# Strided multiplications of an attention and two-MLP kernel: from two engines by a planner's choice to GpSimd, but for one query step of one tile

## The chip, the cores and the metric

One core of one Trainium2 chip runs the whole program. The metric is device time in microseconds (us) for one execution; the number given for a kernel is the median of several executions. Beside it stands one profiled execution, in which the hardware profiler recorded every instruction with its start, its duration and what released it. The engines are TensorE (PE, with its weight loads PEld), VectorE (DVE), ScalarE (ACT), GpSimd (POOL) and the DMA queues, issued here by SyncE (SP).

## The reference: what is computed

Attention over 4 batches, 8 heads, 576 positions, 64 features, and then two gated MLPs (512 to 1536 to 512) over all 2304 tokens. Half of the heads see a local window of 32 positions, the other half a stride: a position sees the earlier positions (and itself) that are congruent to it modulo 32.

```python
mask_local = (rel >= 0) & (rel < stride)                     # heads 0 to 3
mask_strided = (rel >= 0) & (pos[None, :] % stride == pos[:, None] % stride)   # heads 4 to 7
attn = softmax(where(mask, scale * q @ k.T, -1e9))
x = (attn @ v), tokens as rows
x = ((x @ w_a) * (x @ w_b)) @ w_out                          # first MLP
out = (sigmoid(x @ w_gate) * (x @ w_val)) @ w_out2           # second MLP
```

## The kernel before

The 576 positions are cut into five tiles, `TILES`: four of 128 positions and one of 64, for all four batches at once. They carry the index `i` from 0 to 4.

**Local heads** (`attention`, one group per tile and batch) run on TensorE: scores (L542), then a softmax of small steps, DVE maximum L554 and its scaling L555, ACT exponentials L560, DVE L566 and L567 for the reciprocal of the sums, normalisation on DVE (L575) or ACT (L573), then TensorE transposes (L583) and the product with the values (L597).

**Strided heads** (`strided`, one call per tile) have too few pairs for TensorE: a query step `j` of a tile is 32 positions of four batches on 128 partitions, and it sees only `n = t0 + j + 1` keys. So the scores of one head and one query step are one elementwise multiplication of 128 x (n x 64) (L745, `mult`) into one of two product buffers (ring `p`), and one DVE reduction along the features (L751), which gives the buffer back. After a softmax on the strip `s` (L770 to L784) the values take the same way: a multiplication by the weights (L808) and a DVE reduction along the keys (L815), and at last a transpose on TensorE (L841) and two copies (L854 ACT, L858 DVE). The tiles i = 1 to 4 have n = 5..8, 9..12, 13..16 and 17..18, four heads each: 32, 32, 32 and 16 multiplications, 112 together. Tile 0 takes two heads at a time and is not touched by the change.

**First MLP, first half** ("the loop"): for each tile `i`, 24 products over 512 tokens (256 in the last tile) on TensorE (L887), followed by an ACT copy (L982) and a DVE product (L907) that also frees the PSUM bank. In loop step `i` the attention groups and `strided(i + 1)` of the next tile are worked off beside these products. During the first step the weights of this MLP are prepared too (ACT L464, L481; DVE L473, L485), during the third and fourth step weights of the next stage (DVE L1104, L1040, L1150).

**The order of all work** is written by a planner, `Plan`. Each operation has an engine or a choice of several, a price in ns for each, a key and dependencies. `Plan.run` takes, again and again, the operation that can start first by these prices, and, where engines can be chosen, the one on which it would end first. What comes out is one fixed sequence of instructions per engine, with semaphores; on the chip each engine works its own sequence off in order. TensorE's position for the transposes L583 among the products L887 is thus fixed by the planned times. Each strided multiplication before the change has both engines to choose from:

```python
ways = ("POOL", "DVE")
def price(n):
    n *= nh * D
    return n * 2.05 + 100, dve(n)          # dve(n) = (n + 66) / 0.96
...
m = add(ways, price(n), mult, [lk, lqs[c], m if first else None], w, take=ring("p"))
```

**Second stages**: the rest of the first MLP and the second MLP (L1202 on TensorE, with sums and splits around it on DVE, ACT and a few on POOL, L1040) follow after the loop, from about 412 us on.

Of the kernel before, what the change touches and what calls it, by code (L numbers as in the profile page):

```python
# [173 lines left out]
class Plan:  # L174
# [38 lines left out]
    def add(self, eng, cost, fn, deps=(), key=0.0, take=(), free=(), size=0):  # L213
        op = Op()
        op.slack = self.slack
        op.eng, op.cost, op.fn, op.key, op.size = eng, cost, fn, key * 1e3, size
        op.deps = [d for d in deps if d is not None]
        op.take, op.free, op.slot, op.end = take, free, {}, None
        op.seq = len(self.ops)
        self.ops.append(op)  # L220
        for ring, owner in free:
            if ring in PLACE:
                taker, i = owner if isinstance(owner, tuple) else (owner, None)
                rings = [allowed for r, allowed in taker.take if r == ring]
                for allowed in rings if i is None else rings[i:i + 1]:
                    size = RINGS[ring][1]
                    for s in allowed:
                        a = PLACE[ring] + s * size
                        self.ends.append((a, a + size, op))
        return op  # L230
# [80 lines left out]
def dve(n):  # L311
    return (n + 66) / 0.96
# [27 lines left out]
def attention_moe_kernel(ctx, tc, qkv, sq, sk, sv, w1, w2, mask, ident, out):  # L340
    nc = tc.nc
    PE, ACT, DVE, POOL = nc.tensor, nc.scalar, nc.vector, nc.gpsimd
# [32 lines left out]
    add, touch = plan.add, plan.touch  # L375
# [281 lines left out]
    def strided(i, key, length, start, war):  # L657
        first = i == 0
        tq, t0 = TILES[i] // STRIDE, i * TB // STRIDE
        n1 = t0 + tq  # L660
        nh = 2 if first else 1
        ways = ("POOL", "DVE")
        x = {"q": {}, "xs": {}, "ps": {}}
        step = [0]

# [1 line left out]
            step[0] += 1  # L667
            return key + length * step[0] / (2 * HL // nh * tq + 4)

        def price(n):  # L670
            n *= nh * D
            return n * 2.05 + 100, dve(n)


        rings = {"q": ("c", F_RING), "strip": ("raw", (0, 1, 2)), "p": ("p", (0, 1))}
# [3 lines left out]
        def place(op, use, w):  # L679
            if first:  # L680
                return at(*op.early)[:, :w]
            return {"c": small, "raw": raw, "qk": qk_buf, "p": product_buf}[rings[use][0]](op)[:, :w]

        def ring(use):
            return [] if first else [rings[use]]
# [26 lines left out]
        def own_tile(op):  # L712

            if first:
                op.early = early_tile()
                touch(op, (), [op.early])
            return op
# [7 lines left out]
        lqs, reds, m = [], [], None  # L725
        for h in range(0, HL, nh):
            c, e = divmod(h, 2)
            if e == 0:
                def load_q(op, c=c):
                    q = place(op, "q", 2 * tq * D)  # L730
                    nc.sync.dma_start(
                        out=q.rearrange("p (h x) -> p h x", h=2),
                        in_=sq[:, 2 * c:2 * c + 2, t0 * D:n1 * D],
                    )
                    x["q"][c] = q.rearrange("p (h t d) -> p h t d", h=2, d=D)

                lqs.append(own_tile(add("SP", 450, load_q, start, key - 10, take=ring("q"),
                                        size=P * 2 * tq * D * 4)))
            lk = own_tile(add("SP", 450, load_strip(sk, "k", h), start, key - 9 + h * length / 8,
                              take=ring("strip"), size=P * nh * n1 * D * 4))  # L740
            for j in range(tq):
                n = t0 + j + 1

                def mult(op, h=h, e=e, j=j, n=n):
                    engine[op.eng].tensor_tensor(  # L745
                        out=product(op, n), in0=x["k", h][:, :, :n, :],
                        in1=x["q"][h // 2][:, e:e + nh, j:j + 1, :].to_broadcast([P, nh, n, D]),
                        op=ALU.mult)

                def reduce(op, h=h, j=j, n=n):  # L750
                    DVE.tensor_reduce(  # L751
                        out=weights_of(h, j, n), in_=x["p", op.deps[0]], op=ALU.add, axis=AX.X)

                w = when()
                m = add(ways, price(n), mult, [lk, lqs[c], m if first else None], w, take=ring("p"))
                reads(own_tile(m), lk, lqs[c])
                free = freed("p", m)
                if j == tq - 1:
                    free += freed("strip", lk) + (freed("q", lqs[c]) if e + nh == 2 else [])
                reds.append(reads(add("DVE", dve(nh * n * D), reduce, [m, fi], w, free=free), m))  # L760
# [28 lines left out]
        w = when()  # L789
# [4 lines left out]
        o5 = add("DVE", dve(ns), normalise, [o4], w, free=[("sm", o1)])  # L794
        for h in range(0, HL, nh):
            c, e = divmod(h, 2)
            lv = own_tile(add("SP", 450, load_strip(sv, "v", h, STEPS[i], "p (h d t) -> p h d t"), start, key - 9 + (h + 4) * length / 8,
                              take=ring("strip"), size=P * nh * n1 * D * 4))
            for j in range(tq):
                n = t0 + j + 1  # L800

                if first and e == 0 and j == 0:
                    xs_at = early_tile()

                def mult(op, h=h, e=e, j=j, n=n, xs_at=xs_at):
                    if e == 0 and j == 0:
                        x["xs"][h // 2] = at(*xs_at)[:, :tq * P] if first else place(op, "q", tq * P)
                    engine[op.eng].tensor_tensor(  # L808
                        out=product(op, n, "p (h d t) -> p h d t"), in0=x["v", h][:, :, :, :n],
                        in1=weights_of(h, j, n).unsqueeze(2).to_broadcast([P, nh, D, n]),  # L810
                        op=ALU.mult)

                def reduce(op, h=h, e=e, j=j, n=n):
                    xs = x["xs"][h // 2].rearrange("p (t h d) -> p t h d", h=2, d=D)
                    DVE.tensor_reduce(  # L815
                        out=xs[:, j, e:e + nh, :], in_=x["p", op.deps[0]], op=ALU.add, axis=AX.X)

                w = when()
                take = ring("p")
                if e == 0 and j == 0:  # L820
                    take += ring("q")
                m = add(ways, price(n), mult, [lv, o5, m if first else own], w, take=take)
                reads(own_tile(m), lv)
                if e == 0 and j == 0:
                    own = m
                free = freed("p", m)
                if j == tq - 1:
                    free += freed("strip", lv)
                    if h + nh == HL:
                        free.append(("s", fi))  # L830
                red = reads(add("DVE", dve(nh * n * D), reduce, [m, own], w, free=free), m)
                if first:
                    touch(red, (), [xs_at])
                parts[c].append(red)
            if e + nh < 2:
                continue

            def transpose(op, c=c):
                x["ps"][c] = bank(op)
                for j in range(tq):  # L840
                    PE.transpose(  # L841
                        x["ps"][c][:, j * P:(j + 1) * P], x["xs"][c][:, j * P:(j + 1) * P], idt)

            def views(c):
                w = TILES[i]
                o = (i % 2) * N2
                return [x["ps"][c][:, :tq * P].rearrange("p (t b r) -> p t b r", b=B, r=STRIDE)] + [
                    xT(y, 2)[:, c, o:o + B * w].rearrange("p (b t r) -> p t b r", b=B, r=STRIDE)
                    for y in range(2)
                ]  # L850

            def high(op, c=c):
                ps, hi, lo = views(c)
                ACT.copy(out=hi, in_=ps)  # L854

            def low(op, c=c):
                ps, hi, lo = views(c)
                DVE.tensor_tensor(out=lo, in0=ps, in1=r32(hi), op=ALU.subtract)  # L858

            tr = add("PE", tq * 109, transpose, parts[c] + [c_id], w,  # L860
                     take=[("bank", tuple(range(8)) if first else (4, 5, 6, 7))], free=freed("q", own))
            if first:
                touch(tr, [xs_at])
            hi = add("ACT", act(tq * P), high, [tr] + war, w)
            lo = add("DVE", dve(tq * P), low, [hi], w, free=[("bank", tr)])
            outs.setdefault(i, {}).setdefault(2 + c, []).append((hi, lo))
# [77 lines left out]
    for i, n in enumerate(TILES):  # L944
        n *= B
        war = reads1[-1:]
        w = [g for g in GROUPS if g.i == i + 1]
# [9 lines left out]
        for k in range(KF):  # L957
# [4 lines left out]
            ring = "c" if last and k % 2 else "g"  # L962
# [476 lines left out]
    for s in range(KS):  # L1439
# [5 lines left out]
        i, k = ((2, 0), (2, 6), (3, 0), (3, 3), (3, 6), (3, 9))[s]  # L1445
# [92 lines left out]
```

## Time and profile before

| | us |
|---|---|
| median of 3 executions | 957.09 (957.0 to 958.74) |
| profiled execution | 956.21 |
| its span, first to last instruction | 954.40 |
| PE busy in the span | 904.0 (95%) |
| DVE busy | 709.2 (74%) |
| ACT busy | 427.3 (45%) |
| POOL busy | 150.9 (16%) |

The span is what the trace shows; 1.81 us of the profiled execution lie around it. Busy shares are means over stages with different limits: the loop, where DVE, POOL and PE work beside each other, and the stages after it, where PE works nearly without a gap. A PE instruction counts as busy from its start to its modelled end. The granted clock is 1.00 at 2.4 GHz and 0.50 at 1.2 GHz, and stands as a mean over a stretch.

### The profile page before, as it was taken

What the parts mean: (1) busy time and instruction counts of PE and PEld (TensorE: products, weight loads), DVE (VectorE), ACT (ScalarE), POOL (GpSimd) and SP (SyncE); (2) the same over time, 40 slices, a digit from 0 to 9 for tenths busy, and PEclk for the clock granted to TensorE, in tenths of its full rate; (3) what the DMA queues carried; (4) which work ended last, traced back from release to release, by engine and by line L of the source; (5) the groups of instructions that cost most, each with busy time, mean ns of one, the idle gap of its engine ahead of it and who ended that gap; (6) DMA issues with size and microseconds to landing.
All of it is one profiled execution on the core that took longest, in us unless ns stands there. A gap on an engine that the chain in (4) does not pass through costs nothing.

```text
span 954.4 us, 14300 instructions
## 1 busy us (share of the span) xinstructions
PE 904.0 (95%) x5170; PEld 826.2 (87%) x5170; DVE 709.2 (74%) x1101; ACT 427.3 (45%) x883; POOL 150.9 (16%) x101
## 2 busy tenths in 40 slices
PE   5898999979888899999999979999999999999998
PEld 3676777767666678999999979999999999999998
DVE  6999799798979984565859997666566656748591
ACT  4655332214132243334537575555566555435351
POOL 4324335452424510000000221000000000000000
PEclk9999999989999999999999999999999999999999
DMA  9576653455357556994343641537366668954401
GB/s 296 186 265 202 208 158 104 153 150 184 102 177 214 185 167 208 390 361 148 137 157 127 228 150 56 198 125 236 133 213 225 198 234 309 400 176 148 155 11 66
DMA packets 95349, 179.91 MB, mean 189 GB/s; under 512 B 9520, under 2 KB 66480, under 8 KB 93616
## 3 DMA queue, kind: packets, MB, share of 16 engines
q1 hardware_dynamic: 94992, 178.80, 56.1%
q8 instruction: 40, 0.66, 0.3%
q10 hardware_dynamic: 288, 0.21, 0.1%
q14 instruction: 29, 0.24, 0.1%
HBM read 120.78 MB, written 58.20 MB: 188 GB/s over the span
## 4 chain that ended last, share of the span: by engine, by line
PE 74%; DVE 14%; issue 4%; DMA 3%; ACT 2%; POOL 2%; SPq 0%; DVEq 0%; ACTq 0%; POOLq 0%
PE bank L1202 55%; PE bank L887 16%; DVE s L751 2%; DVE rest L815 2%; DVE w9p L745 1%; DVE h16p L907 1%; PE bank L583 1%; DVE rest L473 1%; DMA rest<-w 1%; POOL w9p L745 1%; PE bank L597 1%; DMA rest<-sq 1%; DMA w10p<-w 1%; PE bank L542 1%; DVE w10p L1104 1%
## 5 line engine op out<-in xcount | busy, mean ns | idle before, releaser
L1214 DVE TENSOR_TENSOR rest<-bank,rest 128x384 f32<-128x384 f32 x96 | 52.8, 554 | 76.5 <-PE bank L1202 44.1
L1220 ACT COPY rest<-bank 128x384 f32<-128x384 f32 x96 | 46.0, 479 | 94.3 <-PE bank L1202 94.0
L808 POOL TENSOR_TENSOR w9p<-rest,s 128x448 f32<-128x448 f32 (+13 forms) x37 | 67.8, 1842 | 90.4 <-DVE rest L815 58.2
L745 POOL TENSOR_TENSOR w9p<-rest 128x384 f32<-128x384 f32 (+11 forms) x30 | 55.2, 1845 | 103.0 <-DVE s L751 52.3
L982 ACT COPY h16p<-bank 128x512 f32<-128x512 f32 (+1 forms) x54 | 30.3, 561 | 70.1 <-PE bank L887 60.5
L751 DVE TENSOR_REDUCE s<-w9p 128x8 f32<-128x512 f32 (+13 forms) x57 | 50.5, 904 | 1.9 <-POOL w9p L745 1.7
L907 DVE TENSOR_TENSOR h16p<-bank,h16p 128x512 f32<-128x512 f32 (+1 forms) x54 | 35.2, 653 | 22.1 <-PE bank L887 17.3
L815 DVE TENSOR_REDUCE rest<-w9p 128x64 f32<-128x320 f32 (+13 forms) x56 | 49.9, 907 | 1.4 <-POOL w9p L808 1.4
L560 ACT ACTIVATE rest<-bank,nm 128x96 f32<-128x96 f32 x56 | 18.3, 339 | 59.3 <-DVE nm L555 53.5
L583 PE MATMUL bank<-idt,rest 128*96 128x128 f32 x56 | 12.2, 324 | 29.2 <-DVE rest L575 20.5
L583 PEld LDWEIGHTS bank<-idt,rest 128*96 128x96 f32 x56 | 7.0, 139 | 35.7 <-issue 15.7
L745 DVE TENSOR_TENSOR w9p<-rest 128x704 f32<-128x704 f32 (+11 forms) x26 | 33.4, 1289 | 6.1 <-DMA rest<-sk 4.4
L1224 ACT COPY bank<-bank 128x384 f32<-128x384 f32 x48 | 22.3, 465 | 25.8 <-PE bank L1202 25.3
L1097 ACT ACTIVATE rest<-rest 128x512 f16<-128x512 bf16 x36 | 28.1, 789 | 6.3 <-DMA rest<-w 6.1
L1049 ACT CAST w10p<-rest 128x768 fp32r<-128x768 f32 (+1 forms) x30 | 23.4, 813 | 16.7 <-DVE rest L1040 16.7
L1421 ACT COPY rest<-bank 128x384 f32<-128x384 f32 x24 | 11.5, 481 | 40.9 <-PE bank L1202 40.9
L1104 DVE SCALAR_TENSOR_TENSOR rest<-rest 128x512 uint32<-128x512 uint32 x36 | 25.4, 708 | 4.7 <-ACT rest L1097 4.7
L1285 DVE TENSOR_TENSOR rest<-bank,rest 128x384 f32<-128x384 f32 x36 | 20.0, 555 | 11.5 <-PE bank L1202 11.2
L1279 ACT ACTIVATE rest<-bank 128x384 f32<-128x384 f32 x36 | 17.8, 493 | 21.1 <-PE bank L1202 21.0
L808 DVE TENSOR_TENSOR w9p<-rest,s 128x768 f32<-128x768 f32 (+10 forms) x19 | 24.3, 1280 | 0.5
L1202 PE MATMUL bank<-w10p,w5p 128*128 128x384 f32 x120 | 23.7, 335 | 0.0
L464 ACT ACTIVATE rest<-rest 128x512 f16<-128x512 bf16 x24 | 18.8, 789 | 7.5 <-DMA rest<-w 7.5
(584 smaller groups left out, 2716.3 us busy)
## 6 DMA issues: line engine op xcount, KB each, us to landing
rest<-w SPq DMA_DIRECT2D x60, 511.8 KB, 4.3
h2d<-rest SPq DMA_DIRECT2D x18, 768.0 KB, 4.4
w1d<-w11p SPq DMA_DIRECT2D x72, 128.0 KB, 1.8
h1d<-h16p SPq DMA_DIRECT2D x36, 192.0 KB, 2.2
w10p<-w SPq DMA_DIRECT2D x12, 511.8 KB, 5.1
rest<-qkv SPq DMA_DIRECT2D x12, 416.0 KB, 4.3
w0p<-h1d SPq DMA_DIRECT2D x12, 384.0 KB, 5.5
w1p<-h1d SPq DMA_DIRECT2D x12, 384.0 KB, 5.8
```

The lines of the kernel that those rows point to most:

```text
L583: PE.transpose(x["t"][:, i * P:(i + 1) * P], blocks(x["e"])[:, i, :], idt)
L745: engine[op.eng].tensor_tensor(out=product(op, n), in0=x["k", h][:, :, :n, :], in1=x["q"][h // 2][:, e:e + nh, j:j + 1, :].to_broadcast([P ...
L751: DVE.tensor_reduce(out=weights_of(h, j, n), in_=x["p", op.deps[0]], op=ALU.add, axis=AX.X)
L808: engine[op.eng].tensor_tensor(out=product(op, n, "p (h d t) -> p h d t"), in0=x["v", h][:, :, :, :n], in1=weights_of(h, j, n).unsqueeze(2 ...
L815: DVE.tensor_reduce(out=xs[:, j, e:e + nh, :], in_=x["p", op.deps[0]], op=ALU.add, axis=AX.X)
L887: PE.matmul(x[tag][:, :n], ww[:, c * P:(c + 1) * P], xx(c), start=(u == 0 and c == chunks[0]), stop=(u == last and c == chunks[-1]),)
L907: DVE.tensor_tensor(out=x["g"], in0=x["b"][:, :n], in1=x["g"], op=ALU.mult)
L982: ga, mu = gated(x, key, n, pa, pb, lambda o, a: ACT.copy(out=o, in_=a), ring)
L1104: DVE.scalar_tensor_tensor(out=u, in0=u, scalar=13, in1=at(*top_at, U32), op0=ALU.logical_shift_right, op1=ALU.bitwise_or)
L1202: PE.matmul(bank_of(where), at(*lhs(a, (0, 1, 0)[q], c), F32R), at(*rhs(b, (0, 0, 1)[q], c), F32R), start=p in OPENS and (q, c) == units[0 ...
L1214: DVE.tensor_tensor(out=at(*o), in0=bank_of("Z"), in1=at(*a), op=ALU.add)
L1220: "ACT", act2(NS), lambda op: ACT.copy(out=at(*o), in_=bank_of("Y")), [ops[after]], key - 20))
```

## The change

In the tiles i = 1 to 4 every strided multiplication is given to POOL alone, at a planned price of 2.5 ns an element and 100 ns, and no longer chosen by the planner. The exception is the second query step (j = 1, n = 14, 896 elements) of tile i = 3, whose eight multiplications (four heads, scores and values) are given to DVE alone. Tile 0 keeps its choice and its prices. Since prices and engines are inputs of the planner, the sequences of all engines are planned anew.

```diff
-        ways = ("POOL", "DVE")
...
-        def price(n):
+        def by(n, j):
+
             n *= nh * D
-            return n * 2.05 + 100, dve(n)
+            if first:
+                return ("POOL", "DVE"), (n * 2.05 + 100, dve(n))
+            return ("DVE", dve(n)) if i == 3 and j == 1 else ("POOL", n * 2.5 + 100)
...
-                m = add(ways, price(n), mult, [lk, lqs[c], m if first else None], w, take=ring("p"))
+                m = add(*by(n, j), mult, [lk, lqs[c], m if first else None], w, take=ring("p"))
...
-                m = add(ways, price(n), mult, [lv, o5, m if first else own], w, take=take)
+                m = add(*by(n, j), mult, [lv, o5, m if first else own], w, take=take)
```

## Rows read from the trace of the kernel before

**Rows 1.** Windows: length, PE, PEld, DVE, ACT, POOL busy (instructions), clock, DMA share, GB/s
```profile
26.00:111.00 85.00, 76.46 (x415) 59.11 (x414) 78.90 (x132) 47.29 (x100) 33.35 (x28) 0.94 0.63 202
111.00:176.00 65.00, 62.72 (x366) 48.23 (x365) 56.88 (x86) 17.58 (x62) 25.07 (x16) 1.00 0.52 157
176.00:281.00 105.00, 92.17 (x504) 72.07 (x503) 94.60 (x120) 28.49 (x82) 38.95 (x19) 0.93 0.47 145
281.00:345.00 64.00, 57.28 (x275) 44.42 (x274) 59.57 (x74) 18.24 (x49) 27.54 (x10) 0.95 0.61 193
...
412.00:954.00 542.00, 533.06 (x3023) 530.79 (x3021) 363.43 (x566) 279.31 (x488) 16.28 (x11) 1.00 0.53 181
```

**Rows 2.** Waits of PE from 26 to 412 us: total, times, longest
```profile
PE bank L583 <- DVE rest L575: 20.5, 6, 4.8
PE bank L583 <- ACT rest L573: 8.7, 4, 4.2
```

**Rows 3.** Timeline of PE around one such wait: start, duration, idle before
```profile
241.94 0.61 PE L887 MATMUL bank<-x13p,w3p 128*128 128x512 f32 x2
246.24 0.96 PE L583 MATMUL bank<-idt,rest 128*96 128x128 f32 x4 [3.69 <-DVE rest L575]
246.85 1.20 PE L887 MATMUL bank<-x12p,w3p 128*128 128x512 f32 x2
```

**Rows 4.** Timeline of DVE and POOL: start, duration, what it is
```profile
189.37 1.99 POOL L745 TENSOR_TENSOR w9p<-rest 128x832 f32<-128x832 f32 x1 [2.22 <-DVE s L751]
...
190.34 0.67 DVE L907 TENSOR_TENSOR h16p<-bank,h16p 128x512 f32<-128x512 f32 x1
...
236.74 2.39 POOL L808 TENSOR_TENSOR w9p<-rest,s 128x1024 f32<-128x1024 f32 x1 [4.07 <-DVE rest L815]
...
237.16 2.00 DVE L555 TENSOR_SCALAR nm<-nm 128x4 f32<-128x4 f32 x1
...
330.36 0.17 DVE L555 TENSOR_SCALAR nm<-nm 128x2 f32<-128x2 f32 x1
```

**Rows 5.** Windows, multiplications L745 alone: DVE busy, POOL busy (instructions)
```profile
26.00:111.00 85.00, 3.33 (x4) 14.57 (x12) 0.94 0.63 202
111.00:176.00 65.00, 9.23 (x10) 9.70 (x6) 1.00 0.52 157
176.00:281.00 105.00, 13.30 (x8) 19.14 (x8) 0.93 0.47 145
281.00:345.00 64.00, 7.50 (x4) 11.77 (x4) 0.95 0.61 193
```

**Rows 6.** The same windows, multiplications L808 alone
```profile
26.00:111.00 85.00, 2.09 (x3) 18.38 (x14) 0.94 0.63 202
111.00:176.00 65.00, 8.73 (x7) 15.05 (x9) 1.00 0.52 157
176.00:281.00 105.00, 11.41 (x8) 18.65 (x8) 0.93 0.47 145
281.00:345.00 64.00, 2.55 (x2) 15.77 (x6) 0.95 0.61 193
```

**Rows 7.** Groups by shape, 26 to 345 us on DVE, all of POOL: busy, mean ns
```profile
L808 DVE TENSOR_TENSOR w9p<-rest,s 128x896 f32<-128x896 f32 x1 | 1.1, 1087 | 0.0
...
L808 POOL TENSOR_TENSOR w9p<-rest,s 128x896 f32<-128x896 f32 x3 | 7.2, 2403 | 19.4 <-DMA rest<-qkv 14.4 <-DVE rest L815 4.9
```

**Rows 8.** Groups by shape on DVE, 26 to 345 us: busy, mean ns, idle before
```profile
L473 DVE SCALAR_TENSOR_TENSOR rest<-rest 128x512 uint32<-128x512 uint32 x23 | 19.9, 868 | 0.7 <-ACT rest L464 0.7
L555 DVE TENSOR_SCALAR nm<-nm 128x4 f32<-128x4 f32 x11 | 6.4, 579 | 0.4
L566 DVE TENSOR_SCALAR nm<-nm 128x4 f32<-128x4 f32 x12 | 4.8, 396 | 0.7 <-ACT rest L560 0.7
...
L485 DVE SCALAR_TENSOR_TENSOR w3p<-rest,w3p 128x512 fp32r<-128x512 f32 x3 | 2.0, 680 | 0.0
```

**Rows 9.** Windows, weight preparation L485 alone: DVE busy (instructions)
```profile
26.00:111.00 85.00, 22.22 (x24) 0.94 0.63 202
```

## The prediction

> **What bounds the kernel now.** I read the windows first, cut where one strided tile ends and the next begins. From 412 us on PE is busy 533.06 of 542 us [rows 1]: no work on DVE or POOL can be worth much there, and the change touches none of it. So the answer lies in the four stretches of the loop, 26 to 345 us. In 111 to 176 PE is busy 62.72 of 65 us at full clock; in the three others it lacks 8.5, 12.8 and 6.7 us, and the granted clock is 0.94, 0.93 and 0.95. The engine that is nearly full there is DVE: 78.90 of 85, 94.60 of 105 and 59.57 of 64 us [rows 1], while POOL works 33.35, 38.95 and 27.54 us. I take DVE for the limit of these three stretches, PE for that of the second.
>
> The waits of PE say through which door: ten waits, 29.2 us, all before the transposes L583, that is for a normalised softmax of the local heads (20.5 us by DVE, 8.7 us by ACT, whose input, in the code, comes from DVE's L567) [rows 2]. TensorE's order is fixed, so a softmax that is later than the planner thought stops it. One such wait stands in the timeline: 3.69 us idle before 246.24, and the pair of products behind it takes 1.20 us where the pair before the wait took 0.61 [rows 3]: the clock fell to its lower level. The clock's shares are 0.06 x 85 + 0.07 x 105 + 0.05 x 64 = 15.7 us [rows 1], in part of idle time that is counted already. What can be won in the loop is therefore at most some 45 us.
>
> Why DVE is late is seen where it works beside POOL [rows 4]. L555, a step on 4 elements, takes 0.17 us alone, but 2.00 us when it starts at 237.16 within a POOL multiplication (236.74, 2.39 us): both end within 0.1 us. L907, which reads PSUM, takes 0.67 us in the middle of a POOL multiplication. So some DVE steps wait until the POOL instruction in flight is done, and all that stands behind them in DVE's sequence waits too; reductions and reads of PSUM don't.
>
> **Part 1: multiplications that leave DVE.** By the windows DVE does 4 + 2, 10 + 7, 8 + 8 and 4 + 2 of them in the tiles 1 to 4, 45 together, and POOL 67 of the 112 (of the three L808 in the first stretch one is the last of tile 0) [rows 5, 6]. Their DVE time: 3.33 + 2.09 - 0.68 = 4.7 us (0.68 for tile 0's, a 512-element step [rows 8]); 9.23 + 8.73 = 18.0; 13.30 + 11.41 = 24.7; 7.50 + 2.55 = 10.0; together 57.4 us. After the change eight remain, in tile 3, of 896 elements at 1.09 us [rows 7] = 8.7 us. DVE is relieved of 48.7 us: 4.7, 18.0, 16.0 and 10.0. The reductions stay as they are.
>
> **Part 2: multiplications that POOL gets.** Net 6, 17, 8 and 6, 37 together. POOL's mean in each stretch is (14.57 + 18.38) / 26 = 1.27 us, 24.75 / 15 = 1.65, 37.79 / 16 = 2.36 and 27.54 / 10 = 2.75 [rows 5, 6], so it gets 7.6 + 28.0 + 18.9 + 16.5 = 71 us more and is busy 41 of 85, 53 of 65, 58 of 105 and 44 of 64 us. That fits, tightest in the second stretch. POOL's time costs nothing by itself while it hides beside the products of TensorE; if that cover were gone, the rival on POOL below says what it costs. Of an instruction of 896 elements POOL needs 2403 ns, DVE 1087 [rows 7].
>
> **Part 3: waits that grow.** POOL is in flight in the loop 190 us instead of 123, so DVE's hindered steps meet it more often. What they lose now, over the undisturbed 0.68 us of L485 and 0.17 us of L555 (for L566 too) [rows 4, 8]: L473 19.9 - 23 x 0.68 = 4.3; L485 22.22 - 24 x 0.68 = 5.9 [rows 9]; L555 6.4 - 11 x 0.17 = 4.5; L566 4.8 - 12 x 0.17 = 2.8 us [rows 8]. The first two, 10.2 us, fall upon the 26 POOL multiplications of tile 1, 0.39 us for each; the last two, 7.3 us, upon all 67, 0.11 us for each. So a POOL multiplication costs DVE 0.11 us where no weights are prepared (tile 2) and about 0.5 us where they are (tile 1; tiles 3 and 4 prepare others, which I price alike). Added: 6 x 0.5 + 17 x 0.11 + 8 x 0.5 + 6 x 0.5 = 12 us. The lower end is 37 x 0.11 = 4 us. The upper end is a hindered step for each added multiplication, which waits for half of it: 71 / 2 = 35 us. I take 12, since it comes from the same steps of the same tiles, only more often hit.
>
> The Trainium skill, page "SBUF — State Buffer", section "SBUF: two separate sides", says that VectorE and GpSimd share a pair of ports as an exclusive lock, held for the whole instruction, and that the loser is blocked fully. L555's 2.00 us agree. By that rule the worst case is each added instruction's whole length in front of a waiting DVE step, as an estimate 71 us instead of the 12 taken, and the change would lose.
>
> **Part 4: the sum.** DVE's net relief is 4.7 - 3 = 1.7 us in tile 1, 18.0 - 1.9 = 16 in tile 2, 16.0 - 4 = 12 in tile 3 and 10.0 - 3 = 7 in tile 4. Not all of it reaches the end. In tile 2 PE lacks only 2.3 us [rows 1]. Elsewhere the planner sees the shorter DVE work too and puts the transposes nearer to their scores, which uses up part of it; what surely shrinks is lateness carried from one softmax to the next. Between nothing and all I take a third: 0.5 (tile 1), 0.5 (tile 2), 4 (tile 3) and 2 (tile 4) = 7 us. The clock comes back in the proportion of the waits, 15.7 x 7 / 29.2 = 4 us, of which I count half, since part of it is idle time counted already: 2 us. 9 us from the profiled execution's 956.2 us (span 954.4 and 1.8 around it) gives 947 us; the median of the runs is 0.9 us above that execution, so 948 against 957.1.
>
> A new plan also moves what it does not mean to move: the clearing of buffers (L1079) queues on POOL behind multiplications, the strips and their DMAs on SP's queue are freed when a multiplication that reads them ends, now later on the slower engine, and the next strip load and all loads planned behind it on that queue move with it. I cost these at nothing: POOL keeps idle time in each stretch [rows 1] and covers them. If that cover is gone (tile 2), it is 2 to 3 us of a strip load's lateness, inside the range.
>
> **Rivals.**
>
> *Lateness goes entirely.* With 49 us less to do, DVE catches up before each softmax, and only each softmax's own waits are left. For it: lateness adds up now, DVE being full at 90% and more. Against it: L555 and L566 lie in the chain itself and are hit more often. If about 20 of the 29.2 us and half of the clock's share as before go: 956 - 25 = 931 us; between this and the likeliest lies 938. Chance 0.14.
>
> *No change.* What DVE is relieved of sits in tile 2, where PE was full, and in the other tiles the waits eat the rest: 957 us. For it: tile 1 had 26 of its 32 multiplications on POOL already, and it waits no less. Within 0.2% (1.9 us), which is about what a measurement here can tell from nothing. Chance 0.12.
>
> *Slower through the lock.* The softmax steps on DVE (L555, L566, and L575) are just of the hindered kind; with POOL in flight 60% of the loop, 190 of 319 us, each of some 14 softmaxes in it meets a POOL instruction more often, for half of 2.4 us. One more hit each is 14 x 1.2 = 17 us on the path of the transposes, less the 9 us of relief: 8 us slower, 965 us. It decides when an added multiplication costs DVE more than 48.7 / 37 = 1.3 us. For it: 2.00 us for L555. Against it: on the whole trace a POOL multiplication costs these two steps only 0.11 us. The skill's lock rule above is the ground of this rival. Chance 0.17.
>
> *GpSimd too late.* In tile 2 POOL would have 53 us of multiplications in 65, in series with the softmax of the strip between them and with waits for DVE; at 0.4 us more for each of 32 that is 66 us. Then the strided half of the next tile's input is late, each later tile starts later, and PE waits before a tile's first product: some 5 us, 961 us. It decides when tile 2's multiplications take more than its stretch. Chance 0.07.
>
> **How the numbers follow.** Likeliest, 948 (941 to 955): 0.50. Entirely without lateness: 0.14. No change: 0.12. Lock: 0.17. GpSimd late: 0.07. Faster by over 0.2%: 0.50 + 0.14 = 0.64; within: 0.12; slower: 0.17 + 0.07 = 0.24. The range reaches from 935, in the middle of the second case, to 963, which leaves out about 0.07 below and 0.11 above: the lower end is also a gain of two thirds instead of one third in tiles 3 and 4 with more clock, the upper end the added waits near 35 us.
>
> **What would show it.** Right: DVE's L745 and L808 only in tile 3, eight of 1.0 to 1.1 us; POOL's busy time about 71 us more, mean durations unchanged; PE's waits before L583 from 29 to some 20 us; the stretch of tile 3 several us shorter, that of tile 2 the same length; from 412 us on the same length. Wrong: L555 and L566 at 1 us and more in the mean, POOL waiting for nothing in tile 2 and the first products of a tile behind L841, or waits of PE of the old size at other places, which would mean that their cause is the planner's distance and not DVE's load.

## The result and the profile after

The changed kernel takes 948.5 us (median of 5, 946.01 to 951.54) against 957.55 us for the kernel before; the ratio is 0.9906 with a 95% interval of 0.988 to 0.9932. The forecast was 948 us. The number was met, but, as the experiments show, by another way than the one that I had worked out.

The lines of the program stand two lower after the change: L745 is L747, L751 is L753, L808 is L810, L815 is L817, L887 is L889, L907 is L909, L1104 is L1106.

The profiled execution (948.5 us, span 946.7) by windows, cut again where a strided tile ends, with the columns of [rows 1]:

```profile
26.00:109.00 83.00, 75.17 (x417) 58.14 (x418) 75.94 (x124) 48.06 (x103) 40.98 (x34) 0.98 0.63 203
109.00:183.00 74.00, 69.39 (x404) 54.47 (x403) 47.85 (x74) 17.51 (x57) 52.55 (x33) 0.95 0.48 141
183.00:283.00 100.00, 93.92 (x509) 73.02 (x507) 88.01 (x112) 29.05 (x84) 56.98 (x27) 0.98 0.50 158
283.00:355.00 72.00, 63.06 (x312) 48.43 (x313) 67.03 (x82) 23.04 (x65) 41.80 (x16) 0.95 0.63 208
```

The stretch of tile 2, the second, is 74 us long in place of 65. POOL is busy 53 us of it, and DVE 47.85 us, in [rows 1] 56.88 of 65. The waits of PE from 26 to 412 us, as in [rows 2]:

```profile
PE bank L583 <- DVE rest L575: 12.8, 6, 3.7
PE bank L583 <- ACT rest L573: 11.1, 5, 4.1
PE bank L597 <- ACT rest L589: 1.5, 2, 0.9
PE bank L843 <- DVE rest L817: 1.1, 1, 1.1
```

Before the transposes 29.2 us of waits have become 23.9. The groups that answer to [rows 7, 8], on DVE from 26 to 355 us (busy, mean ns):

```profile
L747 DVE TENSOR_TENSOR w9p<-rest 128x896 f32<-128x896 f32 x4 | 8.8, 2211 | 0.1
L566 DVE TENSOR_SCALAR nm<-nm 128x4 f32<-128x4 f32 x12 | 8.4, 702 | 0.6 <-ACT rest L560 0.5
L555 DVE TENSOR_SCALAR nm<-nm 128x4 f32<-128x4 f32 x11 | 6.8, 618 | 0.4
L810 DVE TENSOR_TENSOR w9p<-rest,s 128x896 f32<-128x896 f32 x4 | 6.3, 1568 | 0.1
```

and of the whole trace the multiplications on POOL (page part 5):

```profile
L747 POOL TENSOR_TENSOR w9p<-rest 128x320 f32<-128x320 f32 (+12 forms) x52 | 94.0, 1828 | 76.6 <-DVE s L753 42.2
L810 POOL TENSOR_TENSOR w9p<-rest,s 128x320 f32<-128x320 f32 (+12 forms) x52 | 96.6, 1881 | 63.3 <-DVE rest L817 36.7
```

Where the time comes from is read off the timeline of PE. Each step of the loop runs from the start of its first instruction L887 to that of the next step's (step 0 from its second one, at 27.1 to 29.4 us); the last column is where the next stage's first product starts. The kernels with an underscore are those of the experiments below:

```
                 step 0   step 1   step 2   step 3   step 4   loop ends at
before            90.6     80.4     94.5     82.7     34.4      411.43
after             88.3     83.7     86.2     83.7     34.4      404.73
e1_tile3          89.9     81.8     85.1     80.1     34.4      400.00
x1_engines        90.2     85.2     92.8     85.3     34.4      417.32
x2_order          88.8     80.4     91.4     82.7     34.4      406.63
b7_nolock         88.5     80.1     91.4     81.3     34.4      402.89
e1_7_nolock       88.8     80.5     78.8     75.5     34.4      386.98
```

Of the 7.7 us between the two spans 6.7 lie ahead of the loop's end: 0.6 before its products, 2.3 in step 0, 8.2 in step 2, while steps 1 and 3 lose 3.4 and 1.0. Behind the loop the program takes 543.0 and 541.9 us.

### The profile page after: what moved, and what is told of

Same layout as the page of the kernel before. It is cut to its first block, busy times and chain, and to the rows that moved or that the text cites. A ratio compares the mean times of both kernels' runs of the same rounds, so it can differ in the third digit from the quotient of the medians.

```text
span 946.7 us, 14276 instructions
## 1 busy us (share of the span) xinstructions
PE 900.0 (95%) x5170; PEld 823.5 (87%) x5170; DVE 691.1 (73%) x1063; ACT 428.2 (45%) x885; POOL 218.3 (23%) x138
## 4 chain that ended last, share of the span: by engine, by line
PE 76%; DVE 11%; DMA 5%; issue 3%; ACT 2%; POOL 2%; SPq 1%; DVEq 0%; POOLq 0%; ACTq 0%
PE bank L1204 55%; PE bank L889 18%; DMA h1d<-h16p 1%; DMA rest<-w 1%; DVE h16p L909 1%; DVE s L753 1%; PE bank L583 1%; PE bank L597 1%; DVE rest L473 1%; DVE rest L817 1%; POOL w9p L810 1%; DVE rest L575 1%; DMA rest<-sk 1%; POOL w9p L747 1%; DVE nm L566 1%
## 5 line engine op out<-in xcount | busy, mean ns | idle before, releaser
L747 POOL TENSOR_TENSOR w9p<-rest 128x320 f32<-128x320 f32 (+12 forms) x52 | 94.0, 1828 | 76.6 <-DVE s L753 42.2
L810 POOL TENSOR_TENSOR w9p<-rest,s 128x320 f32<-128x320 f32 (+12 forms) x52 | 96.6, 1881 | 63.3 <-DVE rest L817 36.7
L753 DVE TENSOR_REDUCE s<-w9p 128x8 f32<-128x512 f32 (+13 forms) x57 | 51.0, 905 | 12.9 <-POOL w9p L747 12.7
L817 DVE TENSOR_REDUCE rest<-w9p 128x64 f32<-128x320 f32 (+13 forms) x56 | 50.4, 910 | 11.2 <-POOL w9p L810 11.0
L909 DVE TENSOR_TENSOR h16p<-bank,h16p 128x512 f32<-128x512 f32 (+1 forms) x54 | 35.3, 653 | 22.9 <-PE bank L889 9.5
L583 PE MATMUL bank<-idt,rest 128*96 128x128 f32 x56 | 11.7, 307 | 24.0 <-DVE rest L575 12.8
L583 PEld LDWEIGHTS bank<-idt,rest 128*96 128x96 f32 x56 | 6.6, 132 | 30.6 <-issue 14.9
L1051 ACT CAST w10p<-rest 128x768 fp32r<-128x768 f32 (+1 forms) x30 | 23.4, 812 | 18.1 <-DVE rest L1042 18.1
L1099 ACT ACTIVATE rest<-rest 128x512 f16<-128x512 bf16 x36 | 28.1, 788 | 6.3 <-DMA rest<-w 6.0
L1423 ACT COPY rest<-bank 128x384 f32<-128x384 f32 x24 | 11.5, 481 | 40.9 <-PE bank L1204 38.2
L1106 DVE SCALAR_TENSOR_TENSOR rest<-rest 128x512 uint32<-128x512 uint32 x36 | 24.5, 685 | 5.3 <-ACT rest L1099 5.3
L1042 POOL TENSOR_TENSOR rest<-w0p,rest 128x384 f32<-128x384 f32 x1 | 1.0, 1016 | 102.2 <-DVE w8p L1053 102.2
L473 DVE SCALAR_TENSOR_TENSOR rest<-rest 128x512 uint32<-128x512 uint32 x24 | 20.8, 870 | 1.1 <-ACT rest L464 1.1
L1149 ACT ACTIVATE w11p<-w11p 128x256 fp32r<-128x256 f32 x24 | 9.9, 416 | 25.5 <-DVE w11p L1042 13.2
```

Source lines behind the costliest of these rows:

```text
L473: DVE.scalar_tensor_tensor(out=u, in0=u, scalar=13, in1=x["t"], op0=ALU.logical_shift_right, op1=ALU.bitwise_or,)
L747: engine[op.eng].tensor_tensor(out=product(op, n), in0=x["k", h][:, :, :n, :], in1=x["q"][h // 2][:, e:e + nh, j:j + 1, :].to_broadcast([P ...
L753: DVE.tensor_reduce(out=weights_of(h, j, n), in_=x["p", op.deps[0]], op=ALU.add, axis=AX.X)
L810: engine[op.eng].tensor_tensor(out=product(op, n, "p (h d t) -> p h d t"), in0=x["v", h][:, :, :, :n], in1=weights_of(h, j, n).unsqueeze(2 ...
L817: DVE.tensor_reduce(out=xs[:, j, e:e + nh, :], in_=x["p", op.deps[0]], op=ALU.add, axis=AX.X)
L909: DVE.tensor_tensor(out=x["g"], in0=x["b"][:, :n], in1=x["g"], op=ALU.mult)
```

## The experiments

The theories. *DVE relief* is that of the prediction: DVE was full, 49 us of multiplications less let it keep up. *Price*: a planned POOL price nearer to the chip's gives a better order. *Reshuffling*, later *order*: the change's worth is that all sequences are planned anew, and the one before was poor. *Distance*: transposes are planned too near to their scores. *Lock in the chain*: the softmax's own small DVE steps, waiting for POOL, make the waits. Each ratio is against runs of the kernel before on the same chip.

**Tile by tile.** `e1_tile3`, `e2_tile2` and `e3_not_tile2` use the new rule for some tiles alone, `e4_price` only the new price:

```diff
-            if first:
+            if first or i != 3:        # e1_tile3; i != 2: e2_tile2; i == 2: e3_not_tile2
                 return ("POOL", "DVE"), (n * 2.05 + 100, dve(n))
...
-            return ("DVE", dve(n)) if i == 3 and j == 1 else ("POOL", n * 2.5 + 100)
+            return ("POOL", "DVE"), (n * 2.5 + 100, dve(n))       # e4_price alone
```

> Only tile i = 3 has the new rule (POOL, but j = 1 on DVE); tiles 1, 2 and 4 choose as before. Theory 'DVE relief, tile by tile': the whole gain sits in the third loop step, whose length fell from 94.5 to 86.2 us, so this kernel has it alone: 949 to 950 us against 957.5. Rival 'price': the gain comes from a planned POOL price that is nearer to the chip, in all tiles; one tile of four gives a quarter to a third of it, about 955 us. Rival 'reshuffling': any new plan moves the time by some us without order, 953 to 961 us.

Measured: 943.61 us, ratio 0.9857 (0.9831 to 0.9883): more than the whole change gives, and not in step 2 alone; step 3, whose tile chose as before, is 2.6 us shorter too.

> Only tile i = 2 has the new rule (all 32 multiplications on POOL). Theory 'DVE relief, tile by tile': PE was full there, relief is worth nothing, and the second loop step gets about 3 us longer as in the changed kernel (80.4 to 83.7 us) with a wait of some 3.7 us before L583: about 960.5 us. Rival 'price': faster, about 955 us. Rival 'reshuffling': 953 to 961 us, with the loss or gain in other steps than the second.

Measured: 951.53 us, ratio 0.9934 (0.991 to 0.9957). Faster, where the relief could be worth nothing; step 1 did get longer (83.1 us), but step 2, with the rule before, got 3.7 us shorter (90.8 us; the profiled execution, 955.27 us, is the slowest of the six).

> The changed kernel, but tile i = 2 chooses as before. Theory 'DVE relief, tile by tile': the loss in the second loop step is avoided and the gains of the others stay: about 945 us, 3 us below the changed kernel. Rival 'price': a part of the gain is lost, about 951 us. Rival 'reshuffling': 943 to 955 us without relation to the steps.

Measured: 945.41 us, ratio 0.9863 (0.9839 to 0.9886), as DVE relief expected, but the loss that it should avoid is there: step 1 takes 85.5 us with the old choice.

> The engines stay the planner's choice, only the POOL price is 2.5 ns an element and 100 ns instead of 2.05. Theory 'DVE relief, tile by tile': the planner now gives DVE more multiplications, not fewer, DVE is fuller and its softmax steps later: 960 to 965 us. Rival 'price': the order fits the chip better, about 950 us.

Measured: 945.29 us, ratio 0.9864 (0.9837 to 0.989). DVE has more multiplications than before (56 of the tiles' 112, not 45), up to the loop's end it is as busy (327.99 us, 327.70 in the kernel before), and the kernel is as fast as the best of these. Its windows of L747 and L810 (DVE busy, POOL busy) in the stretch from 176 to 281 us:

```profile
176.00:281.00 105.00, 10.99 (x9) 17.36 (x7) 0.97 0.48 147
...
176.00:281.00 105.00, 11.29 (x10) 16.01 (x6) 0.97 0.48 147
```

19 of 32 on DVE, and yet a step 2 of 86.0 us. DVE relief as the cause falls with this run. The effects of single tiles don't add up either, and show in steps that were not touched.

**Price or any new order.** `n1_210` and `n2_200` change one digit of the kernel before; `e5_price205` is the changed kernel with the old price; `m1_800` gives the planner 400 ns more for each hop in the local softmax:

```diff
-            return n * 2.05 + 100, dve(n)
+            return n * 2.10 + 100, dve(n)      # n1_210;  n * 2.00 + 100: n2_200
...
-            ... else ("POOL", n * 2.5 + 100)
+            ... else ("POOL", n * 2.05 + 100)  # e5_price205, in the changed kernel
...
-M1, M2 = 400, 50
+M1, M2 = 800, 50                               # m1_800
```

> The kernel before with one number changed: the planned POOL price 2.10 instead of 2.05 ns an element, engines still the planner's choice. Theory 'price' (the gain grows as the planned price nears the chip's): a ninth of the way to 2.5, 956 us. Theory 'DVE relief': a few multiplications more on DVE, 957.5 us or a little above. Theory 'reshuffling' (the sequence before is one of many that differ by chance in how their waits before L583 fall, and it is a poor one): several us away from 957.5, anywhere from 944 to 960 us.

Measured: 947.82 us, ratio 0.9878 (0.9865 to 0.9892).

> The kernel before with the planned POOL price 2.00 instead of 2.05 ns an element. Theory 'price': away from the chip's, 958 to 960 us. Theory 'DVE relief': a few multiplications more on POOL, 956 to 957 us. Theory 'reshuffling': several us away from 957.5 without regard to the direction, 944 to 960 us.

Measured: 957.75 us, ratio 0.998 (0.9968 to 0.9991).

> The changed kernel, the same engines for every multiplication, but the POOL price as before, 2.05 ns an element. Theory 'DVE relief': the engines make the gain, 948 us. Theory 'price': the gain goes, 957 us or more, since each multiplication is planned to end 0.3 us too early. Theory 'reshuffling': 944 to 960 us.

Measured: 948.83 us, ratio 0.9886 (0.9873 to 0.99). A price that is nearer to the chip's is not it: the old price with the new engines is as good as the changed kernel, and 2.5% on the price of the kernel before, with engines still chosen, gives more than 1% of time. The waits of `n1_210`:

```profile
PE bank L583 <- ACT rest L573: 11.6, 7, 3.6
PE bank L583 <- DVE rest L575: 10.9, 5, 3.4
```

22.5 us in place of 29.2, though DVE does as much work: 327.74 us up to the loop's end, 327.70 in the kernel before. `n2_200` gains almost nothing, so not every new order helps: the times scatter from 944 to 958 us, and the sequence before stands at their slow end.

> The kernel before with one number changed: the slack M1 that the planner adds to each hop between engines in the local heads' softmax is 800 ns instead of 400, so that the transposes L583 are planned some 2 us later behind more products of TensorE. Theory 'distance' (what costs time is TensorE standing at a transpose that was planned nearer than the chip's softmax takes, with the low clock behind it, not a full DVE): waits before L583 fall from 29 to 12 us, 940 to 945 us. Theory 'DVE relief': DVE is full, the wait moves elsewhere, 955 to 958 us.

Measured: 955.68 us, ratio 0.9957 (0.9944 to 0.9971). TensorE had more work between scores and transposes, 40 instructions L887 in place of 28 for the softmax whose scores end at 200 us, but it still waited 7.2 us there: from scores to transposes it was 17.6 us in place of 11.5. DVE's sequence fills the room with other steps. The waits before L583 are 25.3 us in all (16.3 and 9.0), where 12 were expected. At this one value, distance fails.

**Engines and order apart.** Both kernels leave the planner alone and only issue the multiplication on another engine than it planned; the sequences of TensorE and ACT, and those of DVE and POOL but for the multiplications, are then, instruction for instruction, those of the kernel whose order they have. `x1_engines` has the order before and the engines after, `x2_order` the reverse:

```diff
-                    engine[op.eng].tensor_tensor(                     # L745 and L808, planner of before
+                    engine["DVE" if i == 3 and j == 1 else "POOL"].tensor_tensor(       # x1_engines, tiles 1 to 4
...
-                    engine[op.eng].tensor_tensor(                     # L747 and L810, planner of after
+                    engine["DVE" if (i, v, h, j) in ON_DVE else "POOL"].tensor_tensor(  # x2_order: the 45 of before
```

> The planner's order of the kernel before, for TensorE, ACT and all other instructions alike, but each strided multiplication of tiles 1 to 4 is issued on the engine that the changed kernel gives it (POOL, but j = 1 of tile 3 on DVE). Engines alone, no new order. Theory 'DVE relief': the engines make the gain, 948 us or a little better. Theory 'order' (the gain is the new order's, whatever the engine): 957 us; if the added POOL time only brings waits, 960 to 970 us.

Measured: 959.17 us, ratio 1.0009 (0.9992 to 1.0027): engines alone are worth nothing. Up to its loop's end, and for the kernel before, the windows say (columns of [rows 1]):

```profile
26.00:417.32 391.32, 356.51 (x1997) 284.69 (x1997) 293.36 (x450) 135.79 (x345) 191.00 (x110) 0.95 0.59 189
```

```profile
26.00:411.43 385.43, 355.05 (x1996) 283.42 (x1994) 327.70 (x485) 135.13 (x345) 124.90 (x73) 0.96 0.60 192
```

DVE is relieved by 34 us, and the loop takes 6 us more in this execution (960.87 us, 1.7 above the median of its kernel; that of the kernel before, 956.21 us, is below its own). The waits of PE are 33.6 us:

```profile
PE bank L583 <- DVE rest L575: 20.0, 6, 6.9
PE bank L583 <- ACT rest L573: 13.6, 4, 6.1
```

And DVE, with less to do, stands before its reductions until POOL's multiplications are done, 44.1 us in the loop (L754 and L818 are here what L751 and L815 are in the kernel before):

```profile
DVE s L754 <- POOL w9p L748: 30.9, 20, 7.4
DVE rest L818 <- POOL w9p L811: 13.2, 18, 1.2
```

In the kernel before it is 3.1 us:

```profile
DVE s L751 <- POOL w9p L745: 1.7, 4, 0.7
DVE rest L815 <- POOL w9p L808: 1.4, 2, 0.8
```

> The planner's order of the changed kernel, but each strided multiplication is issued on the engine that it had in the kernel before (45 on DVE, 67 on POOL). Order alone, old engines. Theory 'order': 948 us. Theory 'DVE relief': 957 us or more, since DVE has its 49 us back and the new order has no room for them.

Measured: 951.37 us, ratio 0.9928 (0.9904 to 0.9952): the order alone brings most of the gain. The rest, from 0.9928 to 0.9906, is within the intervals.

**What a softmax waits for.** `b7_nolock` and `e1_7_nolock` take two small steps of each local softmax off DVE; the addition of 1e-9 to the sums is left out of the computation. `b7_nolock` has the order of the kernel before, `e1_7_nolock` that of `e1_tile3`:

```diff
-            DVE.tensor_scalar_mul(x["nm"], x["nm"], -SCALE)     # L555
...
+            ACT.mul(x["nm"], x["nm"], -SCALE)                   # ahead of the exponentials
...
-            DVE.tensor_scalar_add(x["sm"], x["sm"], 1e-9)       # L566
```

> The kernel before in its own order; of the local heads' softmax the scaling of the maxima (L555) is issued on ACT instead of DVE and the addition of 1e-9 to the sums (L566) is left out, so that no step on 2 or 4 elements of a softmax can wait for a POOL multiplication; the normalisation L575 stays. Theory 'lock in the chain' (these waits, 10.8 us in the kernel before, make the waits before L583 and the low clock behind them): 944 to 949 us. Theory 'DVE is full': only the work itself goes, 20 x 0.3 us of it, 954 to 957 us.

Measured: 950.24 us, ratio 0.9912 (0.9886 to 0.9938): as much as the whole change, in the order of the kernel before, and a little above the 944 to 949 us of the theory. In its profiled execution (946.38 us, the fastest of the six) the waits before the transposes are still 26.9 us (15.2, 7.2 and 4.5) in place of 29.2. They are shorter where L555 was held for 2.00 and 1.88 us: 1.30 in place of 3.69 us at 240.44 (246.24 in the kernel before) and 0.51 in place of 2.52 at 294.37 (303.50). Where it was held for 1.78 us the wait stays, 4.54 in place of 4.30 at 265.61 (272.74), and others grow, such as 5.87 in place of 4.84 at 208.30 (211.37).

> The same edit of the softmax (scaling on ACT, addition of 1e-9 left out) in the kernel with the new rule in tile 3 alone, which took 943.6 us, in that kernel's own order. Theory 'lock in the chain': 936 to 940 us. Theory 'DVE is full': 942 to 944 us.

Measured: 931.16 us, ratio 0.972 (0.9697 to 0.9744), the fastest kernel of the study, and faster than expected; `e1_tile3`, whose order it has, stands at 0.9857. Its waits (L582, L574 and L572 are L583, L575 and L573), and its loop by windows, with that of `e1_tile3` ahead of it:

```profile
PE bank L582 <- DVE rest L574: 9.6, 4, 3.4
PE bank L582 <- ACT rest L572: 2.4, 3, 0.9
```

```profile
26.00:400.00 374.00, 350.98 (x1995) 279.02 (x1994) 318.29 (x474) 137.19 (x352) 140.96 (x81) 0.98 0.61 198
```

```profile
26.00:386.98 360.98, 345.05 (x1993) 276.47 (x1994) 304.78 (x443) 140.69 (x368) 142.48 (x81) 0.99 0.64 205
```

PE lacks 15.9 us in place of 23.0, and for as many instructions it is busy 345.05 us in place of 350.98, at a clock of 0.99 and not 0.98. The waits before the transposes fall from 18.8 to 12.0 us. In `e1_tile3` the two small steps hold DVE for 18.1 us (10.36 and 7.71), while 0.17 us for each of 31 would be 5.3. Both kernels take the steps out whole; how much of the gain is the holding by POOL, and how much that two steps less stand in the softmax, no run tells apart.

## Why the prediction was right in its number, and wrong in a step

**Bound and door: right.** All but 1.0 of the 7.7 us lies before 412 us, and it goes through the waits before L583 and the clock behind them. PE works as much in each kernel; before and after differ in the loop by 2.9 us of idle time (30.4 and 27.5) and 3.8 us of PE busy time (355.05 and 351.27 us), which is the clock.

**Parts 1 and 2: sizes nearly right.** POOL got 94.0 + 96.6 = 190.6 us in place of 123, 68 us more where I had worked out 71. DVE has its eight multiplications of 896 elements, but they take 2211 and 1568 ns and not the 1087 ns of the single one in [rows 7], 15.1 us in place of 8.7: they too wait for POOL. The relief was 57.4 - 15.1 = 42 us, not 48.7.

**Part 3: right in kind, but not by so much for each multiplication.** Up to the loop's end L555 and L566 take 15.93 us in the kernel before and 21.52 us in the changed one, 10.7 and 16.3 us above 0.17 us a step. The means of 0.69 and 0.70 us stay under the 1 us that would have shown the lock rival right. Of these 5.6 us the 37 added multiplications alone bring 2.1 (`x1_engines`, 17.99 us), 0.06 us each; the new order, with no multiplication added, brings 5.3 (`x2_order`, 21.20 us), each in one execution. The 0.11 us of the prediction left out the steps of 2 elements, three of L555 and three of L566 with 2.7 and 1.8 us; with them it is 10.7 / 67 = 0.16 us. And POOL's 190 us in flight should by its own terms, 123 + 71, have been 194. Over all steps of DVE the loop of `x1_engines` has 48 us less of multiplications and 34 us less of busy time, so the others grew by 14 us, near the 12 of the sum; in the changed kernel it is 42 and 18 us, so they grew by 24.

That the two steps are on the path is seen in `b7_nolock` and `e1_7_nolock`, which take them off DVE in an unchanged order and are faster; that it is their holding is argued from its size, not shown by itself. The Trainium skill, page "SBUF — State Buffer", section "SBUF: two separate sides", says of the lock that the loser blocks fully; the 2.00 us of L555 and the eight multiplications above agree. The worst case that the prediction drew from it, each added instruction's whole length on DVE's path, did not come: `x1_engines`, which has all of them, is not slower than the kernel before.

**Part 4 is the step that failed.** "Between nothing and all I take a third" assumed that DVE's relief reaches PE, and Part 2 let POOL's longer time cost nothing by itself. `x1_engines` shows otherwise: 34 us less on DVE, no gain, and 44.1 us in which DVE stands before a reduction for POOL, 3.1 before. DVE's sequence is fixed, so what stands behind such a reduction waits with it; no run takes these waits away by themselves. By tiles the forecast was 0.5, 0.5, 4 and 2 us; the steps of the changed kernel gave 2.3, -3.4, 8.2 and -1.0. That the sum was met is chance. In the order before, some of PE's waits shrink by the relief and others grow. The one of [rows 3] is 0.67 us in `x1_engines`, 3.69 before; the longest grows. In the kernel before:

```profile
209.77 0.99 DVE L751 TENSOR_REDUCE s<-w9p 128x13 f32<-128x832 f32 x1
210.68 0.55 DVE L575 TENSOR_TENSOR rest<-rest,nm 128x384 f32<-128x384 f32 x1
...
211.37 1.06 PE L583 MATMUL bank<-idt,rest 128*96 128x128 f32 x4 [4.84 <-DVE rest L575]
```

In `x1_engines` L555 is held for 2.19 us, where it took 0.17, and the reduction ahead of L575 waits 1.69 us for POOL:

```profile
210.15 2.19 DVE L555 TENSOR_SCALAR nm<-nm 128x4 f32<-128x4 f32 x1
...
216.76 1.02 DVE L754 TENSOR_REDUCE s<-w9p 128x13 f32<-128x832 f32 x1 [1.69 <-POOL w9p L748]
217.69 0.55 DVE L575 TENSOR_TENSOR rest<-rest,nm 128x384 f32<-128x384 f32 x1
...
218.39 1.06 PE L583 MATMUL bank<-idt,rest 128*96 128x128 f32 x4 [6.90 <-DVE rest L575]
```

Which feature of an order makes it good stays open. Single places don't tell: where the changed kernel has no wait at all before the transposes at 262.65 us (4.30 us in the kernel before, at 272.74), `x2_order`, with the same order and most of the gain, waits 4.82 us at 264.46. `n1_210` has a good order and `n2_200` has not, and their prices differ by 5%.

**The rivals.** "Lateness goes entirely" did not come from relief. "No change" is what the engines alone do. "GpSimd too late" had its condition: tile 2 takes 74 us, where the prediction expected the same length as before, 65. But what it should bring is only a transpose L843 at 283.96 us that waits 1.1 us for the last reduction of tile 3; the 3.7 us of wait in step 1, at 127.77 us, stand before the transposes of a local softmax. What I did not list is the case that came true: the change does what it says to the engines, and pays by the order that the planner happens to write.

## What to carry to other kernels

Where a planner writes every engine's sequence, a change of prices or engines is two changes; issue the work on the new engine in the old order, and on the old engine in the new order, before saying which of the two paid. An engine with less to do is not an engine that is done sooner: in a fixed sequence it waits where the work now comes from a slower one. Time single steps in the chain that the bounding engine waits for, however small: in an unchanged order two steps on 2 or 4 elements were worth 0.9%, and 37 multiplications moved nothing. And measure how far the time scatters when a price moves by a few per cent, since a gain of 1% may be that scatter.

## What the runs showed of the hardware that was not expected

L567, a reciprocal on the same 2 or 4 elements of SBUF between L566 and the normalisation, takes 0.15 to 0.18 us in all the timelines here, also within a POOL multiplication, while L566 in front of it takes up to 2.20 us (`m1_800`, at 303.12): of two small DVE steps on the same tile only one is held up. In the changed kernel two POOL multiplications follow each other from 237.83 to 242.10 us; L566 lasts until the first is about done, and L567 runs within the second:

```profile
237.83 4.27 POOL L810 TENSOR_TENSOR w9p<-rest,s 128x832 f32<-128x832 f32 x2 [5.74 <-ACT rest L560]
238.14 1.76 DVE L566 TENSOR_SCALAR nm<-nm 128x4 f32<-128x4 f32 x1 [0.54 <-ACT rest L560]
239.93 0.18 DVE L567 RECIPROCAL nm<-nm 128x4 f32<-128x4 f32 x1
```

And DVE is not the only loser. In three places of these traces preparing steps follow each other without a gap, and POOL appears to wait for all of them. Of the timeline of the changed kernel:

```profile
266.10 4.12 POOL L810 TENSOR_TENSOR w9p<-rest,s 128x1024 f32<-128x1024 f32 x1 [4.49 <-DVE rest L817]
266.21 0.41 DVE L1152 SCALAR_TENSOR_TENSOR w8p<-w10p,w8p 128x256 fp32r<-128x256 f32 x1
...
267.55 0.41 DVE L1152 SCALAR_TENSOR_TENSOR w11p<-w11p 128x256 fp32r<-128x256 f32 x1
267.89 0.68 DVE L909 TENSOR_TENSOR h16p<-bank,h16p 128x512 f32<-128x512 f32 x1
268.49 2.02 DVE L1042 TENSOR_TENSOR w11p<-w10p,w11p 128x256 f32<-128x256 f32 x1
```

Five preparing steps run from 266.21 to 267.96 without a delay. The multiplication, which takes 2.4 us elsewhere, takes 4.12 and ends 2.3 us after the last of them; the next step of the kind, L1042 at 268.49, which takes 0.41 us alone, ends only 0.3 us after it. The other two places are `e2_tile2` at 225.48 (3.72 us for 960 elements, 2.3 elsewhere) and `e3_not_tile2` at 308.05 (4.67 us for 1088 elements, 2.5 elsewhere).
